# Two-stage attention and a feed-forward layer in one kernel: the last two chunks' first product by seven half-size products

## The chip, the cores and the metric

The kernel runs on one core of a Trainium2 chip. The time is the device time of one execution in microseconds; before and after are compared by the median of several executions.

## The reference

The attention output of eight batches, eight heads of 64 and 576 tokens (a pooled attention over groups of four tokens, repeated, plus a local attention in a window of plus or minus three) is the input of a feed-forward layer:

```python
x = attn_out.transpose(0, 2, 1, 3).reshape(4608, 512)
h = x @ w_in                                   # 512 x 2048
g = where(h >= 1, h, where(h <= -1, 0, (h + 1)**2 / 4))
return g @ w_out                               # 2048 x 512
```

Inputs, weights and output are float32.

## The kernel before, in words

Every float32 operand of a feed-forward product is kept as two rounded words, high and low, whose sum is the number; a product is three matmuls, high with high, low with high, high with low. The input x is held in `xh` and `xl`, four blocks of 128 channels by a ring of 1536 tokens; the weights stay in SBUF as `w_i` and `w_o`, 16 blocks of 128 hidden units each.

The 4608 tokens are cut into chunks (`CHUNKS`): one of 512, eight of 384 and two of 512, numbered 0 to 10. A step (c, f) is chunk c and hidden block f. Its first product (`mm1`, `product`, L840) runs over four channel blocks, 12 matmuls as wide as the chunk, into one PSUM bank `ffn_h`. Its gate (`gate`) is a chain over three engines: ScalarE copies the bank to `m` (L859), VectorE makes `u` (L860), ScalarE squares it (L863), VectorE combines (L866), ScalarE rounds to `gh` (L873), GpSimd takes the difference `gl` (L876). Its second product (`mm2`, `second_product`, L894) adds three matmuls of 512 columns for each 128 tokens of the chunk into banks `ffn_o`, and after f = 15 the banks are copied out (L902) and stored.

Steps run in the order of (c, f); the second product of a step follows the first product of the step two later. Chunk 0 and the weight conversion stand in an order written by hand (`ORDER`). Chunks 1 to 8 run in a loop over n, the step's number 16 c + f, and at the numbers in `JOINS` one attention group (`join`: two heads of one batch) is put in, spread over n, n + 1 and n + 2: scores and values on TensorE, softmax on VectorE, ScalarE and GpSimd, two moves of probabilities through the SP queue. A last loop runs chunks 9 and 10. A scheduler orders each engine's instructions by priority (`tc.high_priority`, `tc.issue_after`, `tc.keep_in_program_order`) and places the temporaries `m`, `u`, `gh`, `gl` and `osb` in ten buffers of 128 x 512 (tag `t512`).

```python
first, second = iter(steps[1:]), iter(steps)
for n in range(NFC + 1, (NMID + 1) * NFC + 1):
    mm1(*next(first))
    if n in JOINS:
        joined = join(SECOND + JOINS.index(n), ps_g)
    if n > NFC + 1 and n != JOINS[1]:
        mm2(*next(second))
```

## Time and profile before

| what | value |
|---|---|
| runs | 910.26, 909.3, 906.82 us, median 909.3 |
| profiled execution | 908.62 us, its span 906.8 us |
| TensorE busy | 98% of the span |
| VectorE, ScalarE, GpSimd busy | 50%, 51%, 39% |
| DMA | 84.06 MB, mean 93 GB/s |
| granted TensorE clock | 1.00 (the 2.4 GHz level) over the span |

The profile records each instruction of each engine; PE is TensorE's matmuls, PEld its weight loads, DVE is VectorE, ACT ScalarE, POOL GpSimd. The recorded length of a matmul reaches beyond the start of the next, so the time of one in a stream is the distance of starts, or the length of a chain's piece divided by its matmuls. Line numbers are those of the kernel before.

### The profile page before, as it was taken

How to read it: one execution, taken by the hardware profiler on the slowest of the kernel's cores; microseconds unless marked ns; L12 is line 12 of the kernel's file. 1: busy time of each engine (PE TensorE's matmuls, PEld its weight loads, DVE VectorE, ACT ScalarE, POOL GpSimd, SP SyncE). 2: the span in 40 equal slices, each digit the busy share in tenths (PEclk: the TensorE clock that was granted, in tenths of full speed). 3: DMA queues.
4: the chain of work that ended last, by engine and by line, in shares of the span. 5: the costliest groups of instructions: out<-in, count | busy, mean ns of one | idle time of the engine just before them, and what ended most of it. 6: DMA issues, size and time to landing. Idle time of an engine off the chain costs nothing.

```text
span 906.8 us, 18666 instructions
## 1 busy us (share of the span) xinstructions
PE 890.9 (98%) x7556; PEld 795.9 (88%) x7556; DVE 457.8 (50%) x880; ACT 459.2 (51%) x983; POOL 356.2 (39%) x340
## 2 busy tenths in 40 slices
...
GB/s 349 115 212 313 125 59 62 85 141 130 87 91 74 75 69 90 114 104 91 91 79 48 90 126 42 91 158 90 87 123 108 56 36 1 0 1 48 1 1 46
DMA packets 43606, 84.06 MB, mean 93 GB/s; under 512 B 4448, under 2 KB 16224, under 8 KB 43520
## 3 DMA queue, kind: packets, MB, share of 16 engines
q1 hardware_dynamic: 43376, 82.82, 26.8%
...
q14 instruction: 27, 0.22, 0.1%
q10 hardware_dynamic: 144, 0.05, 0.0%
...
## 4 chain that ended last, share of the span: by engine, by line
PE 79%; DVE 1%; ACT 1%; POOL 0%; issue 0%; DMA 0%; DVEq 0%; ACTq 0%; POOLq 0%
PE ffn_o L894 36%; PE ffn_h L840 35%; PE score_ps L640 2%; PE value_ps L664 1%; PE turn_ps L766 1%; PE value_ps L622 1%; PE local_ps L763 1%; PE score_ps L608 1%; PE value_ps L608 1%; DVE u L866 0%; POOL sl L691 0%; DMA pooled<-sp 0%; DVE u L860 0%; ACT sp L717 0%; ACT m L859 0%
## 5 line engine op out<-in xcount | busy, mean ns | idle before, releaser
L876 POOL TENSOR_TENSOR gl<-u,gh 128x384 fp32r<-128x384 f32 (+1 forms) x176 | 194.0, 1102 | 463.6 <-ACT gh L873 406.5
L840 PE MATMUL ffn_h<-xh,w_i 128*128 128x384 f32 (+1 forms) x1408 | 367.9, 344 | 2.9 <-DVE u L866 2.1
L894 PE MATMUL ffn_o<-w_o,gh 128*128 128x512 f32 x1152 | 346.5, 383 | 0.0
L840 PEld LDWEIGHTS ffn_h<-xh,w_i 128*128 128x128 f32 x1408 | 252.4, 189 | 22.8 <-ACT m L859 3.4
L840 PE MATMUL ffn_h<-xl,w_i 128*128 128x384 f32 (+1 forms) x704 | 240.2, 341 | 0.5 <-POOL xl L553 0.5
L894 PEld LDWEIGHTS ffn_o<-w_o,gh 128*128 128x128 f32 x1152 | 212.6, 189 | 25.3 <-issue 0.6
L860 DVE TENSOR_SCALAR u<-m 128x384 f32<-128x384 f32 (+1 forms) x160 | 73.8, 461 | 304.2 <-ACT m L859 304.2
L894 PE MATMUL ffn_o<-w_o,gl 128*128 128x512 f32 x576 | 218.7, 380 | 0.4 <-POOL gl L876 0.4
L863 ACT ACTIVATE u<-u 128x384 f32<-128x384 f32 (+1 forms) x176 | 97.3, 553 | 113.2 <-DVE u L860 113.2
L873 ACT CAST gh<-u 128x384 fp32r<-128x384 f32 (+1 forms) x176 | 95.7, 544 | 108.5 <-DVE u L866 106.9
L859 ACT COPY m<-ffn_h 128x384 f32<-128x384 f32 (+1 forms) x160 | 80.4, 502 | 122.2 <-PE ffn_h L840 120.5
L840 PEld LDWEIGHTS ffn_h<-xl,w_i 128*128 128x128 f32 x704 | 133.3, 189 | 5.9 <-POOL xl L553 0.8
L866 DVE SCALAR_TENSOR_TENSOR u<-m,u 128x384 f32<-128x384 f32 (+1 forms) x160 | 94.4, 590 | 83.6 <-ACT u L863 83.6
L894 PEld LDWEIGHTS ffn_o<-w_o,gl 128*128 128x128 f32 x576 | 109.1, 189 | 16.0 <-POOL gl L876 0.8
L715 ACT ACTIVATE sl<-sl 128x640 f32<-128x640 f32 x24 | 17.7, 738 | 59.4 <-POOL sl L691 59.4
L578 POOL TENSOR_TENSOR xl<-x,xh 128x576 fp32r<-128x576 f32 (+4 forms) x32 | 35.3, 1109 | 17.9 <-ACT xh L577 17.8
L820 POOL TENSOR_TENSOR w_o<-m,w_o 128x512 fp32r<-128x512 f32 x16 | 25.2, 1586 | 33.0 <-ACT w_o L816 33.0
L691 POOL TENSOR_TENSOR sl<-sl,mxl 128x640 f32<-128x640 f32 x24 | 30.2, 1260 | 2.4 <-DVE mxl L690 1.9
L820 POOL TENSOR_TENSOR w_i<-m,w_i 128x512 fp32r<-128x512 f32 x16 | 21.6, 1356 | 11.7 <-ACT w_i L816 11.7
L741 POOL TENSOR_TENSOR vq_sb<-vq_sb 128x384 f32<-128x384 f32 x24 | 24.3, 1012 | 0.0
L730 DVE TENSOR_REDUCE sums<-sl 128x10 f32<-128x640 f32 x24 | 19.7, 820 | 8.3 <-ACT sl L715 8.3
L622 PE MATMUL value_ps<-ap,vd 128*64 128x144 f32 (+1 forms) x192 | 21.3, 298 | 0.1
...
## 6 DMA issues: line engine op xcount, KB each, us to landing
...
out<-osb SPq DMA_DIRECT2D x36, 256.0 KB, 2.4
raw_i<-w_in SPq DMA_DIRECT2D x16, 512.0 KB, 9.0
raw_o<-w_out SPq DMA_DIRECT2D x16, 512.0 KB, 8.2
...
```

What stands on the lines that cost most here:

```text
L578: nc.gpsimd.tensor_tensor(xl[:, p, dst], x[:, part], xh[:, p, dst], op=ALU.subtract)
L622: put(nc.tensor.matmul(pp_v[hs, :], vd[ks, hs] if main else vd[ks, P : P + D], ap[ks, 0 if main else 1, :, h, :], start=main, stop=not mai ...
L691: shifted = nc.gpsimd.tensor_tensor(slf, slf, ml.unsqueeze(2).broadcast_to([P, NB, WIN]), op=ALU.subtract)
L820: nc.gpsimd.tensor_tensor(w[:, 1], raw[name, f, "m"], w[:, 0], op=ALU.subtract)
L840: ins = nc.tensor.matmul(htiles[c, f], wi[:, wt, cc * P : (cc + 1) * P], turns(xt[:, cc, ts]), start=(cc == 0 and xt is xh and wt == 0), s ...
L859: nc.scalar.copy(m, h)
L860: nc.vector.tensor_scalar(utiles[c, f], m if c > 0 else h, -1.0, 1.0, op0=ALU.max, op1=ALU.add)
L863: nc.scalar.activation(u, u, AF.Square, scale=0.5)
L866: nc.vector.scalar_tensor_tensor(u, utiles["m"] if c > 0 else h, 1.0, u, op0=ALU.max, op1=ALU.min)
L873: nc.scalar.copy(gh, utiles[c, f])
L876: nc.gpsimd.tensor_tensor(gl, utiles.pop((c, f)), gh, op=ALU.subtract)
L894: ins = nc.tensor.matmul(o, gt[:, ts], turns(weights["o", f][:, wt, :]), start=f == 0 and n == 0, stop=f == NFC - 1 and n == 2,)
```

## The change

For chunks 9 and 10 (`LATE` and the next) the first product of two hidden blocks at a time, 256 by 512 weights with 512 by 512 tokens, is split in halves in all three directions, and done by seven products of half size instead of eight, each over 256 channels (two blocks of 128, six matmuls) and 256 columns (`strassen`). The first pair of chunk 9 stays as it was, so 15 pairs take the new form. Four of the seven use sums of weight blocks and four use sums of token blocks:

- Sums of weights are made from high plus low on VectorE in sixteen steps of the middle (`weight_sum`, at the numbers in `SUMS`), rounded to words again one step later on ScalarE and GpSimd (`weight_words`) and stored to DRAM. For each pair they are loaded into the 512 ring places that chunks 9 and 10 don't use (`weight_sums`, `rest`), four loads of 256 KB.
- Sums of tokens of chunk 9 are made on VectorE at the end of the middle (`token_sums`), rounded in the next two steps (`token_parts`, `token_rest`); those of chunk 10 are made between the pairs of chunk 9.
- In `strassen` partial results are added on the way out of PSUM: three ScalarE copies and four VectorE sums of 256 columns, and one GpSimd sum, which build `m` for both blocks; the gate then starts from `m` without the copy L859.
- The last five numbers of `JOINS` become 124, 128, 132, 136, 140 instead of 125, 130, 134, 138, 142. The attention's pool is closed before the last loop, and its place is used for the token sums.

```diff
@@ -139,10 +139,12 @@
...
+SUMS = [35, 41, 42, 47, 48, 55, 56, 61, 71, 83, 89, 90, 95, 96, 103, 104]
+LATE = len(CHUNKS) - 2
 SECOND = 2 * NPAIR
 NALL = B * NPAIR
-JOINS = [17, 20, 23, 26, 30, 37, 44, 51, 58, 63, 68, 73, 78, 85, 92, 99, 106, 111, 115, 120, 125]
-JOINS += [130, 134, 138, 142]
+JOINS = [17, 20, 23, 26, 30, 37, 44, 51, 58, 63, 68, 73, 78, 85, 92, 99, 106, 111, 115, 120, 124]
+JOINS += [128, 132, 136, 140]
...
@@ -851,24 +856,25 @@
     def gate(c, f, piece):
 
         size = CHUNKS[c][1]
-        h = htiles[c, f]
+        h = htiles.get((c, f))
         if piece == "u1":
             utiles[c, f] = temp("u")[:, :size]
-            if c > 0:
+            if (c, f) in summed:
+                m = utiles["m"] = summed[c, f]
+            elif c > 0:
                 m = utiles["m"] = temp("m")[:, :size]
-                nc.scalar.copy(m, h)
+                utiles["copied"] = nc.scalar.copy(m, h)
             nc.vector.tensor_scalar(utiles[c, f], m if c > 0 else h, -1.0, 1.0, op0=ALU.max, op1=ALU.add)
         elif piece == "sq":
             u = utiles[c, f]
             nc.scalar.activation(u, u, AF.Square, scale=0.5)
         elif piece == "u2":
             u = utiles[c, f]
-            nc.vector.scalar_tensor_tensor(
+            utiles["last"] = nc.vector.scalar_tensor_tensor(
                 u, utiles["m"] if c > 0 else h, 1.0, u, op0=ALU.max, op1=ALU.min
             )
         elif piece == "gh":
-            gh = mpool.tile([P, 512], F32R, name="gh", tag="t512", bufs=10)[:, :size]
-            gl = mpool.tile([P, 512], F32R, name="gl", tag="t512", bufs=10)[:, :size]
+            gh, gl = (temp(x, F32R)[:, :size] for x in ("gh", "gl"))
             gtiles[c, f] = gh, gl
             nc.scalar.copy(gh, utiles[c, f])
         else:
@@ -906,6 +912,135 @@
...
+    def halves(x):
+        return x.rearrange("p (a x b) -> p x a b", a=2, x=2)
+    def vector_sum(out, a, b, op):
+        return nc.vector.scalar_tensor_tensor(out, a, 1.0, b, op0=ALU.mult, op1=op)
+    def parts(raw, high, low, on):
+        nc.scalar.copy(high, raw)
+        if on is nc.vector:
+            vector_sum(low, raw, high, ALU.subtract)
+        else:
+            on.tensor_tensor(low, raw, high, op=ALU.subtract)
+    kept = {}
+    def weight_sum(f, k):
+        if k == 0:
+            kept[f] = dram.tile([P, 4, 2, 2, P], F32, name=f"kept{f}", tag=f"kept{f}")
+        r = temp("sums").rearrange("p (i h c) -> p i h c", i=2, h=2)
+        for i in (1, 0):
+            w = weights["i", f + i].rearrange("p t (h k c) -> p t h k c", h=2, k=2)[:, :, :, k]
+            vector_sum(r[:, i], w[:, 0], w[:, 1], ALU.add)
+        a11, a12, a21, a22 = (r[:, i, h] for i in range(2) for h in range(2))
+        vector_sum(a22, a21, a22, ALU.add)
+        vector_sum(a21, a11, a21, ALU.subtract)
+        vector_sum(a11, a22, a11, ALU.subtract)
+        vector_sum(a12, a12, a11, ALU.subtract)
+        return r
+    def weight_words(f, k, r):
+        words = [temp("words", F32R) for _ in range(2)]
+        parts(r.rearrange("p i h c -> p (i h c)"), *words, nc.gpsimd)
+        for t in range(2):
+            nc.sync.dma_start(kept[f][:, :, t, k], words[t].bitcast(F32).rearrange("p (s c) -> p s c", s=4))
+    def rest(i):
+        return xh[:, i, ring(NT) :] if i < NCC else xl[:, i - NCC, ring(NT) :]
+    def weight_sums(f):
+        for i in (3, 0, 1, 2):
+            nc.sync.dma_start(rest(i).bitcast(F32), kept[f][:, i].rearrange("p t k c -> p (t k c)"))
+    def token_sums(pool, c, k, tags):
+        ts = slice(ring(CHUNKS[c][0]), ring(CHUNKS[c][0]) + CHUNKS[c][1])
+        ra, rb = (pool.tile([P, 512], F32, name=f"sums{i}", tag=tags[i]) for i in range(2))
+        for r, i in ((ra, k), (rb, k + NCC // 2)):
+            vector_sum(r, xh[:, i, ts], xl[:, i, ts], ALU.add)
+        b11, b12, b21, b22 = (halves(r)[:, x] for r in (ra, rb) for x in range(2))
+        vector_sum(b11, b12, b11, ALU.subtract)
+        vector_sum(b12, b22, b12, ALU.subtract)
+        vector_sum(b22, b22, b11, ALU.subtract)
+        vector_sum(b21, b21, b22, ALU.subtract)
+        return b11, b12, rb
+    def token_parts(c, k, sums, first, second):
+        b11, b12, rb = sums
+        to = [t.rearrange("p (a k b) -> p k a b", a=2, k=2)[:, k] for t in first]
+        parts(b11, *to, nc.gpsimd)
+        parts(rb, second[2 * k], second[2 * k + 1], nc.vector)
+    def token_rest(c, k, sums):
+        ts = slice(ring(CHUNKS[c][0]), ring(CHUNKS[c][0]) + CHUNKS[c][1])
+        parts(sums[1], halves(xh[:, k, ts])[:, 1], halves(xl[:, k, ts])[:, 1], nc.gpsimd)
+    def strassen(pool, c, f, first, second):
+        ts = slice(ring(CHUNKS[c][0]), ring(CHUNKS[c][0]) + CHUNKS[c][1])
+        a, b, d, e = (banks[x][:, 0:256] for x in ("h0", "h1", "h2", "h3"))
+        def own(i, k0):
+            return lambda t, k: weights["i", i][:, t, (k0 + k) * P : (k0 + k + 1) * P]
+        def of_sums(i):
+            return lambda t, k: rest(i)[:, t * 256 + k * P : t * 256 + (k + 1) * P]
+        def tokens(k0, x):
+            return lambda t, k: halves((xh, xl)[t][:, k0 + k, ts])[:, x].rearrange("p a b -> p b a")
+        def turned(x):
+            return lambda t, k: halves(second[2 * k + t])[:, x].rearrange("p a b -> p b a")
+        def turned_first(t, k):
+            return first[t].rearrange("p (a k b) -> p k b a", a=2, k=2)[:, k]
+        def multiply(ps, left, right, more=False):
+            for k in range(2):
+                for wt, xt in ((0, 0), (1, 0), (0, 1)):
+                    ins = nc.tensor.matmul(
+                        ps, left(wt, k), right(xt, k),
+                        start=not more and k == 0 and wt == xt,
+                        stop=k == 1 and xt == 1,
+                        skip_group_check=True,
+                    )
+                    if k == 0 and wt == xt:
+                        tc.keep_in_program_order(ins)
+        m1, m2 = temp("m"), temp("m")
+        summed[c, f], summed[c, f + 1] = m1, m2
+        both = pool.tile([P, 512], F32, name="both", tag="both", bufs=1)
+        u, p5 = both[:, 0:256], both[:, 256:]
+        with tc.high_priority(offset=100):
+            multiply(a, own(f, 0), tokens(0, 0))
+            nc.scalar.copy(u, a)
+            multiply(d, of_sums(3), turned_first)
+            nc.scalar.copy(p5, d)
+            multiply(b, of_sums(0), turned(1))
+            nc.vector.tensor_tensor(u, b, u, op=ALU.add)
+            multiply(a, own(f, 2), tokens(2, 0), True)
+            utiles["copied"] = nc.scalar.copy(m1[:, 0:256], a)
+            multiply(d, of_sums(1), tokens(2, 1), True)
+            nc.vector.tensor_tensor(m1[:, 256:], d, u, op=ALU.add)
+            multiply(e, of_sums(2), tokens(0, 1))
+            nc.vector.tensor_tensor(u, e, u, op=ALU.add)
+            nc.gpsimd.tensor_tensor(m2[:, 256:], u, p5, op=ALU.add)
+            multiply(b, own(f + 1, 2), turned(0))
+            nc.vector.tensor_tensor(m2[:, 0:256], b, u, op=ALU.add)
+        gates(c, f)
+        gates(c, f + 1)
 
     banks = {}
 
@@ -961,6 +1096,17 @@
     steps = [(c, f) for c in range(1, len(CHUNKS)) for f in range(NFC)]
     first, second = iter(steps[1:]), iter(steps)
     banks.clear()
+    end = ExitStack()
+    turned = {}
+    def places_of(c):
+        if c not in turned:
+            tags = range(6) if c == LATE else range(6, 8)
+            tiles = [end_pool.tile([P, 512], F32R, name=f"turned{t}", tag=f"turned{t}") for t in tags]
+            turned[c] = tiles + ([] if c == LATE else [rest(NCC + t) for t in range(4)])
+        return turned[c][0:2], turned[c][2:]
+    sums_left = [(f % NFC, k) for f in range(2, NFC + 2, 2) for k in range(2)]
     with psum("ps_g") as ps_g, ExitStack() as four:
         single(four, ["o0", "o1"], ["h0"], ["o2"])
         pooled_sums(SECOND)
@@ -979,14 +1125,46 @@
                 mm2(*next(second))
             if n - 2 in JOINS and n - 2 != JOINS[0]:
                 next(joined, None)
+            if n == LATE * NFC - 1:
+                attention.close()
+                end_pool = end.enter_context(tc.tile_pool(name="end", bufs=1))
+                with tc.issue_after(utiles["last"].ins):
+                    tags = ("turned6", "turned7"), ("sums0", "sums1")
+                    sums = [token_sums(end_pool, LATE, k, tags[k]) for k in range(2)]
+            elif n == LATE * NFC:
+                with tc.issue_after(utiles["copied"].ins):
+                    for k in range(2):
+                        token_parts(LATE, k, sums[k], *places_of(LATE))
+            if n - 1 in SUMS:
+                with tc.issue_after(utiles["copied"].ins):
+                    weight_words(*sums_left[SUMS.index(n - 1)], sums)
+            if n in SUMS:
+                with tc.issue_after(utiles["last"].ins):
+                    sums = weight_sum(*sums_left[SUMS.index(n)])
         mm2(*next(second))
     banks.clear()
-    with ExitStack() as end:
-        single(end, ["h0", "h1", "o0", "o1"], ["o2"], ["o3"])
-        mm1(*next(first))
-        for c, f in first:
-            mm1(c, f)
-            mm2(*next(second))
+    with end:
+        single(end, ["h0", "h1", "o0", "o1"], ["o2"], ["o3"], ["h2"], ["h3"])
+        pairs_left = [(i, f) for i in (LATE, LATE + 1) for f in range(0, NFC, 2)][1:]
+        weight_sums(2)
+        mm1(LATE, 1)
+        with tc.issue_after(utiles["copied"].ins):
+            for k in range(2):
+                token_rest(LATE, k, sums[k])
+        mm2(*next(second))
+        for n, (c, f) in enumerate(pairs_left):
+            strassen(end_pool, c, f, *places_of(c))
+            if n + 1 < len(pairs_left):
+                weight_sums(pairs_left[n + 1][1])
+            if c == LATE and f in (4, 8):
+                with tc.issue_after(utiles["last"].ins):
+                    sums = token_sums(end_pool, c + 1, f // 8, ("sums0", "sums1"))
+            elif c == LATE and f in (6, 10):
+                with tc.issue_after(utiles["copied"].ins):
+                    token_parts(c + 1, f // 8, sums, *places_of(c + 1))
+                    token_rest(c + 1, f // 8, sums)
+            for _ in range(2 if n else 1):
+                mm2(*next(second))
         for c, f in second:
             mm2(c, f)
```

TensorE in chunk 10, before: the first product of a block (L840) and the start of a second product (L894); `ffn_h_8768` is a bank of the first product, `ffn_o_8778` and `ffn_o_8769` two of the second.

```order
L840 MATMUL ffn_h_8768<-xh,w_i_1232 128x512 x2
L840 MATMUL ffn_h_8768<-xl,w_i_1232 128x512
...
L894 MATMUL ffn_o_8778<-w_o_1260,gh 128x512 x2
L894 MATMUL ffn_o_8778<-w_o_1260,gl 128x512
```

The same place in the change, from the third of the seven products of a pair to the second products; `ffn_h_9019`, `9020`, `9034` and `9038` are the four banks, `w_i_1049` and `w_i_1147` the pair's own weights, `xh` without `w_i` the loaded sums.

```order
L1013 MATMUL ffn_h_9020<-xl,xh 128x256 x6
L1013 MATMUL ffn_h_9019<-xh,w_i_1049 128x256 x2
L1013 MATMUL ffn_h_9019<-xl,w_i_1049 128x256
...
L1013 MATMUL ffn_h_9034<-xh 128x256 x2
L1013 MATMUL ffn_h_9034<-xl,xh 128x256
...
L1013 MATMUL ffn_h_9038<-xh 128x256 x2
L1013 MATMUL ffn_h_9038<-xl,xh 128x256
...
L1013 MATMUL ffn_h_9020<-xl,w_i_1147 128x256 x6
L900 MATMUL ffn_o_9030<-w_o_1036,gh 128x512 x2
L900 MATMUL ffn_o_9030<-w_o_1036,gl 128x512
```

For a pair, 24 matmuls of 512 columns in two stretches, a second product behind each, became 42 of 256 columns in one stretch, with the second products of two blocks behind it.

ScalarE at the change-over, before: the gate of step (9, 0), the three output copies of chunk 8, and the gate of (9, 1).

```order
L859 COPY m<-ffn_h_1950 128x512
L863 ACTIVATE u<-u 128x512
L873 CAST gh<-u 128x512
L902 COPY osb<-ffn_o_1945 128x512
L902 COPY osb<-ffn_o_1946 128x512
L902 COPY osb<-ffn_o_1954 128x512
L859 COPY m<-ffn_h_8768 128x512
L863 ACTIVATE u<-u 128x512
L873 CAST gh<-u 128x512
```

The same in the change, from the output copies on; `turned` and `xh` are rounded token sums, `both` the first copy out of the half-size products (L1028).

```order
L908 COPY osb<-ffn_o_1947 128x512
L908 COPY osb<-ffn_o_1948 128x512
L926 CAST turned_8984<-sums_8942 128x512
L908 COPY osb<-ffn_o_1956 128x512
L866 COPY m<-ffn_h_9020 128x512
L926 CAST xh<-sums_8933 128x2x128
L926 CAST xh<-sums_8941 128x2x128
L870 ACTIVATE u<-u 128x512
L879 CAST gh<-u 128x512
L1028 COPY both<-ffn_h_9019 128x256
```

Between the output copies and the gate of (9, 1) there are now roundings of token sums, and the first half-size product's copy stands behind that gate's rounding.

VectorE at one of the sixteen steps of the middle, in the change; before, the rows L866 and L860 of one step and the next follow each other here.

```order
L873 SCALAR_TENSOR_TENSOR u<-m,u 128x384
L922 SCALAR_TENSOR_TENSOR sums<-w_i_822 128x256
L922 SCALAR_TENSOR_TENSOR sums<-w_i_682 128x256
L922 SCALAR_TENSOR_TENSOR sums<-sums 128x128 x4
L867 TENSOR_SCALAR u<-m 128x384
L873 SCALAR_TENSOR_TENSOR u<-m,u 128x384
```

The six sums stand behind the step's last gate operation and ahead of the next step's first.

## Rows read from the trace of the kernel before

**Rows 1.** The page: TensorE's share, and the chain that ended last by line.
```profile
PE 890.9 (98%) x7556; PEld 795.9 (88%) x7556; DVE 457.8 (50%) x880; ACT 459.2 (51%) x983; POOL 356.2 (39%) x340
...
PE ffn_o L894 36%; PE ffn_h L840 35%; PE score_ps L640 2%; PE value_ps L664 1%; PE turn_ps L766 1%; PE value_ps L622 1%; PE local_ps L763 1%; PE score_ps L608 1%; PE value_ps L608 1%; DVE u L866 0%; POOL sl L691 0%; DMA pooled<-sp 0%; DVE u L860 0%; ACT sp L717 0%; ACT m L859 0%
```

**Rows 2.** Busy time by stage: middle, change-over, last two chunks.
```profile
core 0: us, PE busy (x) PEld busy (x) DVE busy (x) ACT busy (x) POOL busy (x), PEclk, DMA share, GB/s
300.00:400.00 100.00, 100.00 (x907) 92.27 (x907) 49.52 (x104) 48.50 (x112) 39.26 (x40) 1.00 0.28 89
730.00:760.00 30.00, 30.00 (x142) 26.49 (x142) 7.21 (x12) 12.05 (x21) 8.52 (x7) 1.00 0.07 27
760.00:790.00 30.00, 30.00 (x140) 26.31 (x140) 6.72 (x12) 11.02 (x18) 6.70 (x6) 1.00 0.00 1
```

**Rows 3.** Pieces of the chain of waits: start us, length us, what, matmuls.
```profile
566.56 1.95 PE ffn_h L840 x12
...
778.56 2.59 PE ffn_h L840 x12
781.15 2.59 PE ffn_o L894 x12
...
895.11 6.49 PE ffn_o L894 x30
```

**Rows 4.** Timeline near 185 us: weight loads, transposes; then the transposes' mean (ns).
```profile
185.31 0.30 PEld L840 LDWEIGHTS ffn_h<-xh,w_i 128*128 128x128 f32 x2
185.58 0.19 PEld L840 LDWEIGHTS ffn_h<-xl,w_i 128*128 128x128 f32 x1
185.75 0.35 PEld L840 LDWEIGHTS ffn_h<-xh,w_i 128*128 128x128 f32 x2
...
184.83 0.68 PE L766 MATMUL turn_ps<-ident_r,pooled 128*128 128x128 f32 x6 [1.19 <-DMA pooled<-sp]
...
L766 PE MATMUL turn_ps<-ident_r,pooled 128*128 128x128 f32 x138 | 15.7, 249 | 1.2 <-DMA pooled<-sp 1.2
```

**Rows 5.** Timeline of a gate of chunk 10: start us, length us, what.
```profile
896.96 0.69 DVE L866 SCALAR_TENSOR_TENSOR u<-m,u 128x512 f32<-128x512 f32 x1 [0.69 <-ACT u L863]
...
897.69 0.62 ACT L873 CAST gh<-u 128x512 fp32r<-128x512 f32 x1 [0.76 <-DVE u L866]
...
898.44 1.27 POOL L876 TENSOR_TENSOR gl<-u,gh 128x512 fp32r<-128x512 f32 x1 [3.91 <-issue]
```

**Rows 6.** Timeline of the change-over: the gates of (8, 15) and (9, 0).
```profile
732.87 0.56 DVE L866 SCALAR_TENSOR_TENSOR u<-m,u 128x384 f32<-128x384 f32 x1 [0.59 <-ACT u L863]
736.48 0.43 DVE L860 TENSOR_SCALAR u<-m 128x512 f32<-128x512 f32 x1 [3.06 <-ACT m L859]
...
738.86 1.55 ACT L902 COPY osb<-ffn_o 128x512 f32<-128x512 f32 x3
...
739.03 1.27 POOL L876 TENSOR_TENSOR gl<-u,gh 128x512 fp32r<-128x512 f32 x1 [3.91 <-ACT gh L873]
```

**Rows 7.** Groups by shape: count, busy us, mean ns, then idle before.
```profile
L866 DVE SCALAR_TENSOR_TENSOR u<-m,u 128x384 f32<-128x384 f32 x128 | 72.2, 564 | 61.4 <-ACT u L863 61.4
L866 DVE SCALAR_TENSOR_TENSOR u<-m,u 128x512 f32<-128x512 f32 x32 | 22.2, 692 | 22.3 <-ACT u L863 22.3
...
L577 ACT CAST xh<-x 128x256 fp32r<-128x256 f32 x4 | 1.7, 416 | 0.0
...
L876 POOL TENSOR_TENSOR gl<-u,gh 128x512 fp32r<-128x512 f32 x48 | 65.5, 1367 | 136.7 <-ACT gh L873 115.9 <-PE ffn_o L894 11.8 <-issue 8.9
L578 POOL TENSOR_TENSOR xl<-x,xh 128x256 fp32r<-128x256 f32 x4 | 2.9, 728 | 0.0
```

**Rows 8.** DMA: the hardware queue (packets, MB, share), issues (KB, us to landing).
```profile
q1 hardware_dynamic: 43376, 82.82, 26.8%
...
out<-osb SPq DMA_DIRECT2D x36, 256.0 KB, 2.4
raw_i<-w_in SPq DMA_DIRECT2D x16, 512.0 KB, 9.0
```

13 lines of the change are left out of this document (8 added, 5 removed).

## The prediction

> **What bounds the kernel now.** I read the page first, for the engine that is busy, then the table by stage, then the chain of waits, and last the records of single matmuls, because the change alters their width. The page gives TensorE 98% of the span, and the chain that ended last is made of the two feed-forward products, 36% and 35% of it [rows 1]. By stage it is plainer: in the middle and in both last chunks TensorE is busy for the whole of each stretch at granted clock 1.00, while VectorE, ScalarE and GpSimd are under half busy, and in the last two chunks VectorE is busy about a fifth of the time [rows 2]. The reader is to see in the chain that nothing but matmuls stands in it there: 12 products of 512 columns take 2.59 us, 12 of 384 columns 1.95 us, one behind the other [rows 3]. So a column taken off TensorE in this stage is time taken off the kernel, as long as nothing makes TensorE wait.
>
> **The main term: narrower and fewer columns.** A pair of hidden blocks in a 512-token chunk costs 24 matmuls now, two stretches of 2.59 us, 5.18 us [rows 3]. After the change it costs 7 half-size products of 6 matmuls, 42 matmuls of 256 columns. What one of those takes no row shows; it is worked out from two sides.
> - If the columns limit: one matmul takes 2.59/12 = 0.2158 us at 512 columns and 1.95/12 = 0.1625 at 384 [rows 3], 0.0533 for 128 columns, so 0.1625 - 0.0533 = 0.109 us at 256. That is the lower bound.
> - If the weight load limits: every matmul here has its own load, recorded at 0.19 us. After an idle array, two loads in a row are recorded as 0.30 us, so the second began 0.30 - 0.19 = 0.11 us after the first; where a 384-column matmul covers it, 0.35 - 0.19 = 0.16 [rows 4]. A load therefore needs about 0.11 us of the array and not 0.19; the transposes of 128 columns even follow at (0.68 - 0.25)/5 = 0.086 us [rows 4]. With the rounding of these rows the upper bound is 0.115 us.
>
> The two limits nearly meet. I take 0.110, next to the row of the loads. Then a pair costs 42 x 0.110 = 4.62 us, 0.56 less than 5.18. Of the 16 pairs of the two chunks the first keeps the old form, so 15 x 0.56 = **8.4 us** less; at 0.109 it is 15 x (5.18 - 4.58) = 9.0, at 0.115 15 x 0.35 = 5.3. Break-even is 5.18/42 = 0.123 us.
>
> The trace shows each load beginning while the matmul before it still streams: 12 of 512 columns follow at 0.216 us though a load alone takes 0.11. The Trainium skill (TensorE: Matmul & The Clock Gate, Part 3, "What overlaps and what doesn't") says that a weight load overlaps a running matmul only where their row groups differ; here all use the full 128 rows, so by it a 256-column step would be 0.11 + 0.11 = 0.22 us. By that rule 512 columns would already cost 0.33, and the trace has 0.216, so the measurement decides, and the rule keeps a small chance below.
>
> **Inside one pair.** In the new order ScalarE must copy the first product out of its bank before the fourth (which adds into the same bank) may start, and the second before the fifth. The first copy has two products' time, 2 x 0.66 = 1.3 us, and 256 columns take ScalarE about 0.4 us (0.416 from SBUF) [rows 7]. The question is what stands ahead of it on ScalarE. With S the end of a pair's seven products and the durations of [rows 5, 7], the gate of its first block has its rounded copy at S + 2.4 us, that of the second at S + 4.4, and the last GpSimd step ends at S + 5.8. The next pair's first product ends at S + 5.18 + 0.66 = 5.84, so the copy finds ScalarE free, and the second products need those gates only after the next pair. GpSimd has one 256-column sum of 0.73 and two 512-column ones of 1.37 per pair [rows 7], 3.5 us of 9.8. VectorE's four sums out of PSUM and four gate steps are about 4 us of 9.8. I cost all of this at nothing; its cover is the pair of second products between two groups, 5.18 us. If that cover failed, the fourth product would be late next.
>
> The transformed weights come back from DRAM in four pieces of 256 KB per pair, each into the place that the pair before read. From the product that frees a place to the one that reads it again lie 6 products and 5.18 us, 9.1 us. A 256 KB store lands in 2.4 us; the slowest row, 512 KB loads issued in a burst, has 9.0 [rows 8]. The queue moved 82.82 MB in 26.8% of the span [rows 8], about 340 GB/s when busy, so 1 MB is 3 us. I take the 2.4, as these loads meet an almost idle DMA (share 0.00 to 0.07 [rows 2]): nothing, with 9.0 as the other end, which still fits.
>
> **The middle.** Sixteen steps get weight sums: on VectorE two of 256 and four of 128 elements, which from 0.564 us at 384 and 0.692 at 512 [rows 7] are 2 x 0.44 + 4 x 0.31 = 2.1 us. They stand behind the step's last gate operation; the next gate operation comes some 2 us later, and it waits at most for this. One step later come a ScalarE copy (0.62) and a GpSimd difference (1.37), both behind that step's own gate, and two stores of 256 KB behind them on SP. A gate at 512 columns is done 899.71 - 895.11 = 4.6 us after its product [rows 3, 5], one at 384 sooner, while its second product is two steps later, 4 x 1.95 = 7.8 us [rows 3]. So over 3 us of delay are covered: nothing, at most 1 us for temporaries that wait for a store to land. On SP the next issues are an attention group's loads, later than the stores in the program; the five groups moved are one or two steps earlier with the same matmuls, and groups four steps apart run already: nothing.
>
> **The change-over.** The token sums of the first of the two chunks stand on VectorE between the last 384-column gate (done at 733.43) and the next gate, which now starts at 736.48 [rows 6]. They take 4 x 0.69 + 4 x 0.44 = 4.5 us, so that gate starts at about 738.0, 1.5 late, and its last GpSimd step ends near 742.1 instead of 740.3 [rows 6]. The second product that needs it starts at 742.14 and wants that operand 0.43 later: just covered. The gate after it is worse: ScalarE has three output copies (1.55 as now [rows 6], now each after 740.8), a rounding of 0.62, and two of 0.42 ahead of its last rounding, which ends near 746.7. Behind that stands the copy of the first half-size product, done at 747.1. TensorE reaches the fourth product at 742.14 + 2.59 + 3 x 0.66 = 746.7: **0.4 us** lost, once; bounds 0 and 2. The tail is unchanged: four copies and stores after the last product; no row shows TensorE waiting there now.
>
> **The sum.** -8.4 + 0.4 = -8.0 us. The profiled execution took 908.62 us (span 906.8), so 900.6; the median of the three runs, 909.3, is 0.7 above it and would give 901.3. I predict **901.0 us**.
>
> **The rivals.**
> - *The load is not hidden* (slower). If a load holds the array for its recorded 0.19 us, a pair is 42 x 0.19 = 7.98, 2.8 more than now, 15 x 2.8 = 42 us, 951. It decides from 0.123 us on. For it speaks that the loads now fill 26.3 of 30 us [rows 2], against it the spacing of 0.11 and the transposes' 0.086 [rows 4]. With the step of 0.22 it would be 15 x 4.1 = 61 us more, 970. Together with values just above break-even 0.08.
> - *A wait in every pair* (no change). If the copy queues behind one more 0.62 us rounding, or a weight piece lands 0.5 us after its 9.1, then 0.3 to 0.6 us per pair go, 15 times 4.5 to 9: 905 to 910. For it speaks that ScalarE and VectorE run in order and the temporaries are ten buffers for up to twelve live tiles; against it that ScalarE is free 1.4 us before it is needed. 0.17.
> - *The middle pays.* If each of the sixteen steps delayed TensorE by 0.2 us, 3.2 us go: 904, still faster. 0.05.
>
> **How the numbers follow.** The forecast, 0.70, lies between 908.6 - 9.0 = 899.6 and 908.6 - 5.3 + 0.4 = 903.7; runs of before differ by some 3 us. The range 898.8 to 906.5 takes in the third rival and the better half of the second and leaves out some 0.2. About 0.5%, 4.5 us, is what a measurement of this kernel can tell from no change. Faster by more: the forecast and the third rival, 0.75; within: the second, 0.17; slower: the first, 0.08.
>
> **What would show it.** In the last two chunks the chain should hold seven groups of six, each near 0.66 us, the mean step 0.109 to 0.111; TensorE busy all through, with at most one idle spot of some 0.4 us at the first fourth product; the middle stretches unchanged; the weight pieces landing in 2 to 4 us. The prediction is wrong if the step is above 0.115 us, if idle time stands before a half-size product with ScalarE, VectorE or a DMA as releaser in each pair, or if the middle has grown.

## The result and the profile after

The change makes the kernel slower: 916.8 us (median of 6 runs, 916.02 to 917.81) against 909.7 us before (6 runs, 906.82 to 910.7), a ratio of 1.0082 with a 95% interval of 1.0067 to 1.0098. Predicted were 901.0 us in a range of 898.8 to 906.5. The profiled execution took 916.02 us, span 914.2 us, 7.4 us longer than the span of before.

The page of the changed kernel: TensorE's busy time, and the chain that ended last by line.

```profile
PE 888.8 (97%) x7826; PEld 796.6 (87%) x7826; DVE 557.5 (61%) x1064; ACT 468.8 (51%) x1026; POOL 395.1 (43%) x379
...
PE ffn_o L900 27%; PE ffn_h L845 21%; PE ffn_h L1013 8%; DVE sums L922 4%; ACT u L870 2%; ACT sp L721 1%; DVE u L873 1%; PE score_ps L644 1%; ACT m L866 1%; DVE u L867 1%; PE turn_ps L770 1%; PE value_ps L668 1%; PE local_ps L767 1%; PE value_ps L626 1%; DMA kept<-words 1%
```

TensorE's busy time is only 2.1 us less than before [rows 1], but now VectorE, ScalarE and even the stores of the rounded sums stand in the chain, where before nearly everything was matmuls. By stage (columns as in [rows 2]):

```profile
300.00:400.00 100.00, 97.31 (x885) 88.11 (x884) 61.05 (x125) 48.22 (x109) 43.24 (x43) 1.00 0.36 113
...
765.00:795.00 30.00, 30.00 (x202) 28.02 (x201) 20.10 (x35) 12.58 (x26) 13.23 (x12) 1.00 0.38 115
795.00:825.00 30.00, 30.00 (x202) 28.02 (x201) 18.04 (x32) 11.77 (x25) 12.03 (x11) 1.00 0.35 106
```

The last two chunks are as full as before; the middle is not: 2.69 us of these 100 TensorE is idle. The granted clock is 1.00 (the 2.4 GHz level) in all of them, so the clock is not the reason. In the chain of waits a pair in the last two chunks reads (start, length, what, matmuls):

```profile
796.17 4.69 PE ffn_h L1013 x42
800.86 5.18 PE ffn_o L900 x24
806.04 4.69 PE ffn_h L1013 x42
```

4.69 us for 42 matmuls is 0.1117 us each; the pair of first products took 2 x 2.59 = 5.18 us before [rows 3]. So the last two chunks gain 0.49 us per pair, 15 x 0.49 = 7.35 us, and the kernel still loses. Where TensorE waited in the middle, and two other waits of the same stretch (260 to 760 us: us in total, times, longest):

```profile
PE ffn_h L845 <- ACT m L866: 6.7, 10, 1.2
...
DVE u L867 <- DMA kept<-words: 4.4, 2, 2.3
...
ACT m L866 <- POOL words L930: 2.9, 2, 1.4
...
PE ffn_o L900 <- ACT osb L908: 2.5, 3, 1.2
```

Before, TensorE had no wait of this kind there. L866 is ScalarE's copy of a first product out of its PSUM bank; all middle first products share one bank, so the next one can't start before that copy.

**An account by places.** The profiled executions differ by up to 8 us ahead of the first product of (1, 9): it starts at 193.3 to 195.6 us where the granted clock shows 1.00 up to there, and at 195.7 to 201.6 us where it shows 0.91 to 0.99 for some stretches in there. From that product on two traces can be laid over each other product by product. The starts of four first products, read from the timelines, and what they give; a loss is the distance between two starts, less that distance before (row 1: 444.59 and 88.99 us):

```
kernel           (1,9)   (7,12)  (8,15)  (9,0)   lost (1,9)-(7,12)  lost (7,12)-(8,15)  (9,0) to the end
before           195.60  640.19  729.18  733.07         -                  -                173.8
after            195.33  651.63  742.12  746.01       11.7                1.5               168.2
joins_only       201.62  646.45  736.95  740.85        0.2                1.5               173.8
before_9         200.62  645.17  734.39  738.28        0.0                0.2               173.8
no_sums          198.11  643.16  733.74  737.64        0.5                1.6               168.2
sums_no_words    194.28  639.78  730.79  734.68        0.9                2.0               168.2
words_no_sums    199.49  650.19  740.72  744.61        6.1                1.5               168.5
not_stored       196.62  650.40  740.99  744.88        9.2                1.6               168.2
diff_on_vector   198.26  649.10  739.84  743.73        6.3                1.8               168.2
spread           196.67  642.85  733.81  737.70        1.6                2.0               168.2
best1            195.31  639.98  729.19  733.08        0.1                0.2               170.6
best2            193.34  638.12  727.34  731.23        0.2                0.2               169.8
best3            198.49  648.07  737.30  741.20        5.0                0.2               167.6
best4            195.68  640.73  730.43  734.32        0.5                0.7               167.6
```

For the change: 11.7 us lost while the sixteen sum steps run, 1.5 us behind them, 5.5 us gained in the last two chunks, 0.3 us of an earlier start: +7.4 us, the whole difference of the spans.

**One stall followed.** Sum steps 103 and 104 stand ahead of the attention group that starts at step 106. VectorE, GpSimd, ScalarE and TensorE of the changed kernel from the timeline near 570 us (start, length, what, idle before and its releaser):

```profile
562.69 0.76 DVE L922 SCALAR_TENSOR_TENSOR sums<-w_i 128x256 f32<-128x256 f32 x2
563.37 2.71 DVE L922 SCALAR_TENSOR_TENSOR sums<-sums 128x128 f32<-128x128 f32 x3
565.99 0.35 DVE L867 TENSOR_SCALAR u<-m 128x384 f32<-128x384 f32 x1
566.26 0.29 DVE L922 SCALAR_TENSOR_TENSOR sums<-sums 128x128 f32<-128x128 f32 x1
...
569.82 0.80 DVE L867 TENSOR_SCALAR u<-m 128x384 f32<-128x384 f32 x1 [2.33 <-DMA kept<-words]
...
571.68 0.82 DVE L688 TENSOR_TENSOR sl<-score_ps,band_sb 128x640 f32<-128x640 f32 x1
...
563.26 1.05 POOL L882 TENSOR_TENSOR gl<-u,gh 128x384 fp32r<-128x384 f32 x1 [2.90 <-issue]
564.28 1.32 POOL L930 TENSOR_TENSOR words<-sums,words 128x512 fp32r<-128x512 f32 x1
...
569.13 1.27 POOL L930 TENSOR_TENSOR words<-sums,words 128x512 fp32r<-128x512 f32 x1
...
574.77 0.74 ACT L719 ACTIVATE sl<-sl 128x640 f32<-128x640 f32 x1 [2.40 <-POOL sl L695]
...
577.04 0.49 ACT L866 COPY m<-ffn_h 128x384 f32<-128x384 f32 x1
...
577.59 0.59 PE L845 MATMUL ffn_h<-xh,w_i 128*128 128x384 f32 x2 [1.17 <-ACT m L866]
```

The same group in the kernel before:

```profile
558.94 0.36 DVE L860 TENSOR_SCALAR u<-m 128x384 f32<-128x384 f32 x1 [2.39 <-ACT m L859]
...
560.37 0.82 DVE L684 TENSOR_TENSOR sl<-score_ps,band_sb 128x640 f32<-128x640 f32 x1
...
563.41 0.74 ACT L715 ACTIVATE sl<-sl 128x640 f32<-128x640 f32 x1 [2.41 <-POOL sl L691]
...
565.68 0.49 ACT L859 COPY m<-ffn_h 128x384 f32<-128x384 f32 x1
...
566.39 0.49 PE L840 MATMUL ffn_h<-xh,w_i 128*128 128x384 f32 x2
```

The first product that runs meanwhile starts 9.86 us later in the change (572.36 against 562.50). Less that, the gate's first step stands at 559.96, 1.0 us late, mostly because its buffer still holds a rounded sum whose store has not landed (the copy that it reads is 0.3 us late, behind the rounding), and takes 0.80 us in place of 0.36, as GpSimd's difference runs beside it. All of the group's work on VectorE is queued behind this gate, so the group's exponential on ScalarE is 1.5 us late (574.77 - 9.86 = 564.91 against 563.41), and the copy of the next first product, queued behind the group's operations on ScalarE, is late by the same (567.18 against 565.68). Before, that copy ended at 566.17, 0.2 us before the product that wants the bank. So TensorE idles, 1.17 us for this group, and loses 1.33 (a 384-column matmul is recorded as 0.33 us, 0.16 longer than the distance to the next one, so each loss is 0.16 us more than the idle time). Of the nine waits for the copy that are 0.18 us or longer, seven stand two steps behind the start of a group; the other two, 1.20 us each, are at ends of chunks. The ten waits make 6.7 + 10 x 0.16 = 8.3 of the 11.7 us; two waits for an output copy at the same two ends of chunks, 0.50 and 0.74 us, are the largest part of the rest. Laid over before product by product, the change loses 0.3 to 0.8 us a few steps behind each sum step that stands singly (35, 61, 71, 83; all two steps ahead of a group), 0.7 or 1.4 us behind each two in a row next to a group (41 and 42, 55 and 56, 89 and 90, 103 and 104), and 2.4 and 2.6 us behind the two in a row at an end of a chunk (47 and 48, 95 and 96): 11.4 us in all. At the end of a chunk the sums meet three output copies as well:

```profile
310.30 1.55 ACT L908 COPY osb<-ffn_o 128x512 f32<-128x512 f32 x3
...
311.73 0.64 ACT L926 CAST words<-sums 128x512 fp32r<-128x512 f32 x1
312.51 1.27 POOL L930 TENSOR_TENSOR words<-sums,words 128x512 fp32r<-128x512 f32 x1 [1.04 <-ACT words L926]
...
313.81 0.48 ACT L866 COPY m<-ffn_h 128x384 f32<-128x384 f32 x1 [1.44 <-POOL words L930]
...
314.34 0.59 PE L845 MATMUL ffn_h<-xh,w_i 128*128 128x384 f32 x2 [1.20 <-ACT m L866]
```

Here the copy itself wants the buffer of the sums, and that comes free only when GpSimd has read it, behind ScalarE's rounding, behind the output copies.

### The profile page after: what moved, and what is told of

It is laid out like the page before. It is cut to its first block, busy times and chain, and to the rows that moved or that the text cites. A ratio compares the mean times of both kernels' runs of the same rounds, so it can differ in the third digit from the quotient of the medians.

```text
span 914.2 us, 19864 instructions
## 1 busy us (share of the span) xinstructions
PE 888.8 (97%) x7826; PEld 796.6 (87%) x7826; DVE 557.5 (61%) x1064; ACT 468.8 (51%) x1026; POOL 395.1 (43%) x379
## 4 chain that ended last, share of the span: by engine, by line
PE 62%; DVE 9%; ACT 6%; issue 2%; DMA 2%; POOL 1%; SPq 0%; DVEq 0%; ACTq 0%; POOLq 0%
PE ffn_o L900 27%; PE ffn_h L845 21%; PE ffn_h L1013 8%; DVE sums L922 4%; ACT u L870 2%; ACT sp L721 1%; DVE u L873 1%; PE score_ps L644 1%; ACT m L866 1%; DVE u L867 1%; PE turn_ps L770 1%; PE value_ps L668 1%; PE local_ps L767 1%; PE value_ps L626 1%; DMA kept<-words 1%
## 5 line engine op out<-in xcount | busy, mean ns | idle before, releaser
L845 PE MATMUL ffn_h<-xh,w_i 128*128 128x384 f32 (+1 forms) x1168 | 297.7, 337 | 11.2 <-ACT m L866 7.1
L845 PEld LDWEIGHTS ffn_h<-xh,w_i 128*128 128x128 f32 x1168 | 206.0, 189 | 29.1 <-ACT m L866 14.9
L845 PE MATMUL ffn_h<-xl,w_i 128*128 128x384 f32 (+1 forms) x584 | 194.3, 333 | 0.5 <-POOL xl L557 0.5
L867 DVE TENSOR_SCALAR u<-m 128x384 f32<-128x384 f32 (+1 forms) x160 | 76.1, 475 | 163.3 <-ACT m L866 158.0
L873 DVE SCALAR_TENSOR_TENSOR u<-m,u 128x384 f32<-128x384 f32 (+1 forms) x160 | 105.4, 659 | 80.6 <-ACT u L870 80.6
L845 PEld LDWEIGHTS ffn_h<-xl,w_i 128*128 128x128 f32 x584 | 110.4, 189 | 2.7 <-POOL xl L557 0.8
L866 ACT COPY m<-ffn_h 128x384 f32<-128x384 f32 (+1 forms) x130 | 62.7, 482 | 56.3 <-PE ffn_h L845 48.1
L922 DVE SCALAR_TENSOR_TENSOR sums<-sums 128x128 f32<-128x128 f32 (+1 forms) x72 | 43.4, 602 | 1.5
L1039 POOL TENSOR_TENSOR m<-both 128x256 f32<-128x256 f32 x15 | 11.5, 767 | 40.1 <-DVE both L1038 34.6
L1032 DVE TENSOR_TENSOR both<-ffn_h,both 128x256 f32<-128x256 f32 x15 | 6.4, 424 | 33.5 <-PE ffn_h L1013 32.5
```

Source lines behind the costliest of these rows:

```text
L845: ins = nc.tensor.matmul(htiles[c, f], wi[:, wt, cc * P : (cc + 1) * P], turns(xt[:, cc, ts]), start=(cc == 0 and xt is xh and wt == 0), s ...
L866: utiles["copied"] = nc.scalar.copy(m, h)
L867: nc.vector.tensor_scalar(utiles[c, f], m if c > 0 else h, -1.0, 1.0, op0=ALU.max, op1=ALU.add)
L873: utiles["last"] = nc.vector.scalar_tensor_tensor(u, utiles["m"] if c > 0 else h, 1.0, u, op0=ALU.max, op1=ALU.min)
L922: return nc.vector.scalar_tensor_tensor(out, a, 1.0, b, op0=ALU.mult, op1=op)
```

## The experiments

Two theories were set against each other first: the sums, their rounding and the ten buffers delay the middle; or the stores and the moved groups do.

**joins_only**, the kernel before with the groups of the change:

```diff
-JOINS = [17, 20, 23, 26, 30, 37, 44, 51, 58, 63, 68, 73, 78, 85, 92, 99, 106, 111, 115, 120, 125]
-JOINS += [130, 134, 138, 142]
+JOINS = [17, 20, 23, 26, 30, 37, 44, 51, 58, 63, 68, 73, 78, 85, 92, 99, 106, 111, 115, 120, 124]
+JOINS += [128, 132, 136, 140]
```

> The kernel before, with the last five attention groups at the steps of the change and nothing else. If the moved groups cost time by themselves, it is slower than before by 1.2 to 1.6 us (the changed kernel's trace falls 1.5 us further behind in the steps past the last weight sum, and shows one wait of TensorE for a copy of an output row there, 1.2 us, at the end of a chunk): about 911 us. If that loss comes from work that the weight sums left behind, it stays at 909.7 us.

Measured: 911.3 us, ratio 1.002 (0.9998 to 1.0041), which alone would not tell it from before. The trace does: 1.5 us lost behind (7, 12), as in the change, and next to nothing (0.2) ahead of it. The group at 128 starts at the end of a chunk:

```profile
PE ffn_o L894 <- ACT osb L902: 1.2, 1, 1.2
```

**no_sums**, the change without sums and rounding:

```diff
-        r = temp("sums").rearrange("p (i h c) -> p i h c", i=2, h=2)
-        for i in (1, 0):
-            w = weights["i", f + i].rearrange("p t (h k c) -> p t h k c", h=2, k=2)[:, :, :, k]
-            vector_sum(r[:, i], w[:, 0], w[:, 1], ALU.add)
-        a11, a12, a21, a22 = (r[:, i, h] for i in range(2) for h in range(2))
-        vector_sum(a22, a21, a22, ALU.add)
-        vector_sum(a21, a11, a21, ALU.subtract)
-        vector_sum(a11, a22, a11, ALU.subtract)
-        vector_sum(a12, a12, a11, ALU.subtract)
-        return r
+        return None
...
-        words = [temp("words", F32R) for _ in range(2)]
-        parts(r.rearrange("p i h c -> p (i h c)"), *words, nc.gpsimd)
         for t in range(2):
-            nc.sync.dma_start(kept[f][:, :, t, k], words[t].bitcast(F32).rearrange("p (s c) -> p s c", s=4))
+            nc.sync.dma_start(kept[f][:, :, t, k], weights["i", f + k][:, t].bitcast(F32).rearrange("p (s c) -> p s c", s=4))
```

> The changed kernel without the sums of the weights and without their rounding; the stores to DRAM stay, as many and as large, but take words of the weights themselves (so the output of the last two chunks is not the reference's). If the sums' arithmetic and its temporaries delay the first products in the middle, the 11.7 us that the middle lost up to the last sum come back: about 905 us. If the stores (their traffic, or their place in SyncE's queue ahead of the attention's loads) are what delays, it stays near 915 us.

Measured: 905.9 us, ratio 0.9954 (0.9939 to 0.9969); lost up to (7, 12): 0.5 us. So the stores' traffic and their place in SyncE's queue cost nearly nothing; the arithmetic and its buffers cost 11.2 of the 11.7 us.

**sums_no_words** has VectorE's sums alone:

```diff
-        words = [temp("words", F32R) for _ in range(2)]
-        parts(r.rearrange("p i h c -> p (i h c)"), *words, nc.gpsimd)
         for t in range(2):
-            nc.sync.dma_start(kept[f][:, :, t, k], words[t].bitcast(F32).rearrange("p (s c) -> p s c", s=4))
+            nc.sync.dma_start(kept[f][:, :, t, k], weights["i", f + k][:, t].bitcast(F32).rearrange("p (s c) -> p s c", s=4))
```

> The changed kernel with VectorE's six sums in every step, but without the rounding on ScalarE and the difference on GpSimd, and with the stores from the weights (the last two chunks' output is not the reference's). If the delay is VectorE's own time, most of the 11.7 us stays: 912 us or more. If the delay is the ring of ten buffers, in which the sums and their two words hold three until the stores land, it falls to about 905 us. Between them (907 to 911) both have a share.

Measured: 905.7 us, ratio 0.9959 (0.9934 to 0.9985); lost 0.9 us. VectorE's own time alone is not what delays. **words_no_sums**, the complement:

```diff
-        r = temp("sums").rearrange("p (i h c) -> p i h c", i=2, h=2)
...
-        vector_sum(a12, a12, a11, ALU.subtract)
+        r = weights["i", f + k][:, 0].bitcast(F32).rearrange("p (i h c) -> p i h c", i=2, h=2)
```

> The changed kernel, at its own steps, without VectorE's sums: ScalarE's rounding, GpSimd's difference and the two stores are kept, on words of the weights in place of the sums (the last two chunks' output is not the reference's). If the rounding step is what delays (ScalarE and GpSimd ahead of the gate, two buffers held until the stores land), it stays near 913 to 917 us. If it takes both, sums on VectorE beside a difference on GpSimd, and a third buffer held from one to the other, then it falls to 904 to 908 us, as the run with sums and no rounding did (905.7 us).

Measured: 910.5 us, ratio 1.0017 (0.9998 to 1.0036); lost 6.1 us. Neither expectation: the rounding alone loses 6.1, the sums alone 0.9, and together they lose more (11.7) than the two apart (7.0). **before_9** asked whether the ring of ten buffers is short:

```diff
-        return mpool.tile([P, 512], F32, name=name, tag="t512", bufs=10)
+        return mpool.tile([P, 512], F32, name=name, tag="t512", bufs=9)
...
-            gh = mpool.tile([P, 512], F32R, name="gh", tag="t512", bufs=10)[:, :size]
-            gl = mpool.tile([P, 512], F32R, name="gl", tag="t512", bufs=10)[:, :size]
+            gh = mpool.tile([P, 512], F32R, name="gh", tag="t512", bufs=9)[:, :size]
+            gl = mpool.tile([P, 512], F32R, name="gl", tag="t512", bufs=9)[:, :size]
```

> The kernel before with nine buffers in the ring of 512-column temporaries in place of ten, and nothing else. If the ring is what the sums run short of (they take up to three of the ten for a step or two), one buffer less in every step shows it with no sums at all: 2 us or more slower than before, with first products that wait for a ScalarE copy. If the ring has buffers to spare, and the sums delay by their own time on VectorE, ScalarE and GpSimd, it stays within 1 us of before.

Measured: 913.6 us, ratio 1.0054 (1.0031 to 1.0077), and yet nothing lost in the middle (0.0 us; TensorE's waits for a ScalarE copy are 0.3 us in all from 240 to 790 us). In its profile, of a run close to the median (913.8), the 5 us stand ahead of (1, 9); as joins_only, with ten buffers, starts as late in its profile, what nine buffers cost the first chunk is left open. For the middle it says that one buffer less is free, so this run doesn't decide about three. **not_stored** asks directly how much the held buffers cost:

```diff
-            nc.sync.dma_start(kept[f][:, :, t, k], words[t].bitcast(F32).rearrange("p (s c) -> p s c", s=4))
+            nc.sync.dma_start(kept[f][:, :, t, k], weights["i", f + k][:, t].bitcast(F32).rearrange("p (s c) -> p s c", s=4))
```

> The changed kernel with all its sums and rounding at its own steps, on the same engines and in the same buffers; only the stores take words of the weights instead of the rounded sums (the last two chunks' output is not the reference's), so that a buffer comes free when ScalarE and GpSimd are done with it and not when a store has landed, 2 to 3 us later. If it is the held buffers that delay the gates, the 11.7 us that the middle lost (trace, up to the last sum) fall to 3 us or less, and the time to about 908 us. If it is the work itself (VectorE's sums, and the lock-step with GpSimd's difference), 9 us or more of the 11.7 stay: 914 us or more.

Measured: 914.4 us, ratio 1.0053 (1.0033 to 1.0072); lost 9.2 us, as expected if it is the work itself. Waiting for the stores to land is 2.5 of the 11.7 us; the group of the stall above loses 0.5 us in place of 1.3. **diff_on_vector** takes GpSimd out:

```diff
-        parts(r.rearrange("p i h c -> p (i h c)"), *words, nc.gpsimd)
+        parts(r.rearrange("p i h c -> p (i h c)"), *words, nc.vector)
```

> The changed kernel with the second word of the sums on VectorE in place of GpSimd. In the changed kernel's trace a sum of 128 columns that takes 0.29 us alone took 0.97 to 1.25 us while GpSimd's difference ran, and ended just behind it. If that blocking is a large part of the loss, the 11.7 us of the middle fall by 3 us or more (VectorE gets 0.7 us of work for a 1.3 us block): about 913 us or less. If the buffers held until the stores land are the cause, the loss stays within 2 us of 11.7.

Measured: 912.6 us, ratio 1.0033 (1.0016 to 1.0049); lost 6.3 us. With the difference away from GpSimd 5.4 of the 11.7 us are gone, though VectorE now has it to do. Groups by shape on VectorE in the change, and then in diff_on_vector (count, busy us, mean ns, idle before):

```profile
L922 DVE SCALAR_TENSOR_TENSOR sums<-sums 128x128 f32<-128x128 f32 x64 | 36.0, 562 | 1.4
...
L922 DVE SCALAR_TENSOR_TENSOR sums<-w_i 128x256 f32<-128x256 f32 x32 | 12.1, 420 | 0.6
```

```profile
L922 DVE SCALAR_TENSOR_TENSOR sums<-sums 128x128 f32<-128x128 f32 x64 | 25.2, 395 | 1.4
L922 DVE SCALAR_TENSOR_TENSOR words<-sums,words 128x512 fp32r<-128x512 f32 x16 | 17.2, 1074 | 20.6 <-ACT words L926 20.6
```

A sum of 128 columns falls from 562 to 395 ns. It was also wrong in my expectation that VectorE would pay 0.7 us for the difference: it takes 1.07 us there, and the kernel is faster with it all the same. This run changes two things at once: the blocking beside GpSimd, and how soon the sums' buffer is read; which share each has is not separated.

**spread** asks whether it is the price of a step or its place:

```diff
-SUMS = [35, 41, 42, 47, 48, 55, 56, 61, 71, 83, 89, 90, 95, 96, 103, 104]
+SUMS = [33, 40, 47, 54, 60, 65, 70, 75, 81, 88, 95, 102, 109, 113, 118, 122]
```

> The changed kernel with its sixteen sum steps at other places: one by one, two or three steps behind the start of an attention group, where after has them by twos just ahead of one. If it is the next group's work on ScalarE and VectorE that has no room for a delay, about half of the 11.7 us comes back or more: 907 to 911 us. If every sum step costs its 0.7 us wherever it stands, it stays at 915 to 917 us.

Measured: 907.6 us, ratio 0.9977 (0.9959 to 0.9994), faster than before; lost 1.6 us. The same work in the same buffers on the same engines costs 1.6 us at these places and 11.7 at those. What is left stands mostly behind 109, 113 and 118 (0.46 us each), which are two steps ahead of a group; the steps with three or more lose next to nothing. The run also takes apart the steps that stood two in a row. That this alone is not the reason shows in the change's four single steps, which lose 0.3 to 0.8 us each, and in a single step at the end of a chunk in best3 below, 3.2 us; whether two in a row cost more than two single steps at such places is left open. **best1** follows this:

```diff
-SUMS = [35, 41, 42, 47, 48, 55, 56, 61, 71, 83, 89, 90, 95, 96, 103, 104]
+SUMS = [33, 40, 47, 54, 60, 65, 70, 75, 81, 88, 95, 102, 108, 117]
...
-JOINS = [17, 20, 23, 26, 30, 37, 44, 51, 58, 63, 68, 73, 78, 85, 92, 99, 106, 111, 115, 120, 124]
-JOINS += [128, 132, 136, 140]
+JOINS = [17, 20, 23, 26, 30, 37, 44, 51, 58, 63, 68, 73, 78, 85, 92, 99, 106, 111, 115, 120, 125]
+JOINS += [130, 133, 137, 140]
...
+            if c == LATE and f in (10, 12):
+                with tc.issue_after(utiles["copied"].ins):
+                    weight_words(0, f // 2 - 5, late)
+            if c == LATE and f in (8, 10):
+                with tc.issue_after(utiles["last"].ins):
+                    late = weight_sum(0, f // 2 - 4)
```

> The changed kernel with three tables changed: fourteen sum steps one by one, each three steps or more ahead of the next attention group; the last two (the sums for the last chunk's first pair) in the last chunk but one, where TensorE does not wait; the last attention groups at steps 125, 130, 133, 137 and 140, away from the end of a chunk at step 128. If the place of the steps decides, the middle is within 0.6 us of before's, and the last two chunks keep their 5.5 us: 904 to 905.5 us, 5 us under before. If every sum step has a price of its own, it stays at or above the 907.6 us of the run with the steps spread.

Measured: 905.4 us, ratio 0.996 (0.994 to 0.998). The middle is level with before's (0.1 and 0.2 us), so place decides for sums and groups alike. But "TensorE does not wait there" was wrong of the last two chunks: the two pairs that got sums take 10.85 and 11.21 us in place of 9.87. **best2** adds one order at the change-over:

```diff
-        mm1(LATE, 1)
+        for cc in range(NCC):
+            product(LATE, 1, cc)
+        with tc.high_priority(offset=100):
+            for piece in ("u1", "sq", "u2"):
+                gate(LATE, 1, piece)
...
-            nc.scalar.copy(u, a)
+            copied = nc.scalar.copy(u, a)
+            if (c, f) == (LATE, 2):
+                with tc.issue_after(copied.ins):
+                    for piece in ("gh", "gl"):
+                        gate(c, 1, piece)
```

> As best1, with one order more: at the change-over ScalarE copies the first half-size product out of its bank ahead of the gate's rounding, not behind it. In the changed kernel that copy came late and TensorE waited 0.8 us for it, and the first pair with one second product took 8.35 us where its matmuls come to 7.28 us. If that order is the cause, 0.8 to 1 us less than best1; if the copies before it in ScalarE's queue (the rounding of the token sums) are late as well, no difference.

Measured: 904.4 us, ratio 0.9953 (0.9933 to 0.9973); by the trace 0.7 us less than best1 from (9, 0) to the end, first pair 7.68 us in place of 8.36. The order was most of that wait. In its pairs with sums it is mostly VectorE that is late (TensorE's waits, 755 to 830 us):

```profile
PE ffn_h L1013 <- DVE both L1036: 1.1, 2, 0.7
PE ffn_h L1013 <- ACT both L1028: 0.4, 1, 0.4
```

**best3** puts all sixteen steps into the middle again:

```diff
-SUMS = [33, 40, 47, 54, 60, 65, 70, 75, 81, 88, 95, 102, 108, 117]
+SUMS = [27, 33, 40, 47, 54, 60, 65, 70, 75, 81, 88, 95, 102, 108, 112, 117]
...
-            if c == LATE and f in (10, 12):
-                with tc.issue_after(utiles["copied"].ins):
-                    weight_words(0, f // 2 - 5, late)
-            if c == LATE and f in (8, 10):
-                with tc.issue_after(utiles["last"].ins):
-                    late = weight_sum(0, f // 2 - 4)
```

> As best2, but all sixteen sum steps in the middle, the last two of them at steps 27 and 112, one step behind the start of a group and three ahead of the next, and none in the last two chunks. In best2 the pairs with those two sums took 0.98 and 1.33 us longer. If a sum step three steps ahead of a group is free, the middle stays within 0.5 us of before's, and the time is 2 us under best2: 902 to 903 us. If one step behind a group's start is too early, each of the two costs about 0.5 us: 903 to 904 us.

Measured: 907.7 us, ratio 0.9975 (0.9959 to 0.9991). A miss: the last two chunks get back their 2.3 us (167.6), but the middle loses 5.0, of which 3.2 us at step 112, at whose rounding the output copies of a chunk stand:

```profile
603.90 0.66 ACT L926 CAST words<-sums 128x512 fp32r<-128x512 f32 x1
...
604.69 1.27 POOL L930 TENSOR_TENSOR words<-sums,words 128x512 fp32r<-128x512 f32 x1 [2.17 <-DMA out<-osb]
605.04 0.59 PE L845 MATMUL ffn_h<-xh,w_i 128*128 128x384 f32 x2 [0.84 <-ACT m L866]
...
606.00 0.36 DVE L867 TENSOR_SCALAR u<-m 128x384 f32<-128x384 f32 x1 [5.09 <-POOL words L930]
```

GpSimd's difference waits 2.17 us for a buffer that an output store still holds, and the gate waits for GpSimd. **best4** moves those two steps:

```diff
-SUMS = [27, 33, 40, 47, 54, 60, 65, 70, 75, 81, 88, 95, 102, 108, 112, 117]
+SUMS = [33, 40, 47, 54, 60, 65, 70, 75, 81, 88, 95, 102, 108, 117, 122, 127]
```

> As best3, with its two bad steps replaced: 27 (one step behind a group's start) and 112 (the step at which a chunk ends) give way to 122 and 127, each two steps behind a group's start and three ahead of the next. In best3's trace the two cost 1.2 and 3.2 us of the 5.0 us that its middle lost. If the place is what costs, the middle is within 0.5 us of before's, the last two chunks are as short as best3's, and the span is 4 to 5 us under best3's at a like start: 902 to 903 us. If sixteen steps in the middle are two too many wherever they stand, 905 us or more.

Measured: 904.1 us (902.54 to 905.05, 6 runs) against 909.6 us (11 runs) of before on the same chip, ratio 0.9938 (0.992 to 0.9956): 0.6% faster than before, 1.4% faster than the change by the two ratios. The time is 1 us above what was expected, as the middle loses 0.5 and 0.7 us. All of its waits for a ScalarE copy from 240 to 760 us, and its sums on VectorE:

```profile
PE ffn_h L845 <- ACT m L866: 0.2, 1, 0.2
```

```profile
L922 DVE SCALAR_TENSOR_TENSOR sums<-sums 128x128 f32<-128x128 f32 x64 | 29.9, 467 | 1.6
L922 DVE SCALAR_TENSOR_TENSOR sums<-w_i 128x256 f32<-128x256 f32 x32 | 12.1, 418 | 0.1
```

The sums are nearly as dear as in the change (42.0 us of VectorE against 48.1); what differs in the middle is the places of sums and groups.

## Why the prediction was wrong

- **The main term: right in its mechanism, a size off.** One matmul of 256 columns takes 0.1117 us, inside my bounds of 0.109 and 0.115; I took 0.110. A pair gains 0.49 us and not 0.56, 7.35 us and not 8.4. The rival that a load holds the array for its recorded 0.19 us is ruled out by that step. By the Trainium skill's rule (TensorE: Matmul & The Clock Gate, Part 3, "What overlaps and what doesn't"), that a load overlaps a running matmul only where their row groups differ, the step would have been 0.22 us; all loads here use the full 128 rows, and the trace has 0.1117.
- **Inside one pair: right, once 0.2 us off.** The first of the fourteen distances between starts of pairs belongs to the change-over (8.35 us, below); of the other thirteen, twelve are 9.87 to 9.91 us, 4.69 + 5.18, and one is 10.07. No wait came in every pair. The weights' sums landed 3.4 us after their issue, not 2.4, still well inside 9.1:

```profile
xh<-kept SPq DMA_DIRECT2D x60, 256.0 KB, 3.4
```

- **The middle: the step that failed.** I wrote "over 3 us of delay are covered: nothing, at most 1 us for temporaries that wait for a store to land". The cover I named is that of a gate's result, which its second product wants two steps later. Nobody waited for that. What came late was the *next first product*, over a path I hadn't followed: gate, then the attention group's work behind it on VectorE and ScalarE, then the copy out of the only bank. Its slack is small next to a group: at the one followed above the trace of before shows 0.2 us (the copy at 565.68 ends at 566.17, and the product that wants the bank starts at 566.39), against the over 3 us that I had counted on the other path, and I never looked at it there. I also took the sums at 2.1 us per step; they take 2 x 0.42 + 4 x 0.56 = 3.1, as half of the 64 sums of 128 columns run beside a GpSimd operation. That rival, "the middle pays", had 0.2 us per step and a chance of 0.05; it was 11.7/16 = 0.73 us. The runs divide the 11.7: stores' traffic at most 0.5 (no_sums), held buffers 2.5 (not_stored), GpSimd's difference 5.4 (diff_on_vector), sums alone 0.9; these overlap and are not a sum. Nearly all of it vanishes with the place (best1, with fourteen of the sixteen steps there: 0.1; best4, with all sixteen: 0.5 and 0.5 more behind (7, 12) than best1).
- **The moved groups: wrong.** "The same matmuls, and groups four steps apart run already: nothing" overlooked where they land: 1.5 us (joins_only), mostly as the group at 128 meets the output copies of a chunk.
- **The change-over: right in the place, too small.** I named the first half-size product's copy behind a gate's rounding on ScalarE, and took 0.4 us. The wait is there, longer:

```profile
758.77 1.18 DVE L873 SCALAR_TENSOR_TENSOR u<-m,u 128x512 f32<-128x512 f32 x1 [0.71 <-ACT u L870]
...
760.04 0.62 ACT L879 CAST gh<-u 128x512 fp32r<-128x512 f32 x1 [1.30 <-DVE u L873]
760.57 0.36 ACT L1028 COPY both<-ffn_h 128x256 f32<-128x256 f32 x1
...
760.98 0.49 PE L1013 MATMUL ffn_h<-xh,w_i 128*128 128x256 f32 x2 [0.80 <-ACT both L1028]
```

  The gate's step on VectorE takes 1.18 us where it takes 0.69 [rows 7], beside GpSimd's difference of token sums. The first pair and one second product take 8.35 us for 4.69 + 2.59 = 7.28, 1.1 more, and 0.3 go ahead of it (758.01 against 752.49 + 5.18). With the 0.2 us above, 1.6 of the 7.35 - 5.5 = 1.8 us are accounted for. Why it is longer stands ahead of that gate, in the term of the token sums, 4 x 0.69 + 4 x 0.44 = 4.5 us: the kernel has eight sums of 256 columns there, not four, and four of the eight take 0.95 to 1.50 us beside GpSimd in place of 0.42. With two gate operations and a difference between them they last from 746.28 to 755.98 us, 9.7 us. The chain of waits leads from the last of them to the late copy (start, length, what):

```profile
754.56 1.43 DVE sums L922
...
756.01 0.62 ACT turned L926
756.63 0.49 ACT osb L908
757.12 0.49 ACT m L866
...
758.77 1.19 DVE u L873
...
760.66 0.28 ACT both L1028
```

  The order of copy and rounding decides whether this reaches TensorE: in best2 the sums take as long and only that order differs, and 0.7 us come back.
- **The sum** was -8.4 + 0.4; it is -7.35 + 1.8 + 11.7 + 1.5 - 0.3 (an earlier start) = +7.4. Without the misplaced steps the same idea is worth its saving: best4, with the order of best2, gains 6.2 us from (9, 0) on, loses 1.2 in the middle, and is 5.5 us under before by the medians.
